# A new order for the same operations of an attention and feed-forward kernel, from the second product with w_in on

## The chip, the cores and the metric

The kernel runs on one core of a Trainium2 chip. The metric is the time of the slowest core in device microseconds, here that of the only core; several runs are taken and their median counts. A core has five engines with an instruction queue each: TensorE (PE, matrix products into PSUM banks), VectorE (DVE), ScalarE (ACT), GpSimd (POOL) and SyncE (SP, which here only issues DMAs).

## The reference

Attention without a softmax over pairs: q is normalised over its 64 elements, k over the 576 positions, and the product k·v of a head (64x64) is multiplied by q. What comes out is the input of a feed-forward layer with a softplus.

```
q_s = exp(q - max(q, -1));  q_s = q_s / (sum(q_s, -1) + 1e-09)        # (8, 8, 576, 64)
k_s = exp(k - max(k, 2));   k_s = k_s / (sum(k_s, 2) + 1e-09)
kv  = einsum('bhsd,bhse->bhde', k_s, v)
x   = einsum('bhsd,bhde->bhse', q_s, kv)  -> (4608, 512)
h   = x @ w_in                                                        # (512, 2048)
g   = maximum(h, 0) + log1p(exp(-abs(h)))
out = g @ w_out                                                       # (2048, 512)
```

## The kernel before

The 4608 tokens are nine tiles t of 512. Two heads are worked on together, so there are four head pairs h for each of the eight batches b. A full-precision product is made of three products of split operands: each operand is a high part (a cast to fp32r, which PE reads) and a low part (what the cast left), and high·high, high·low and low·high are added up in one PSUM bank. So a 128x512 product stands on PE three times in a row (L595 to L597 with w_in, L637 to L639 with w_out).

The work is cut into units, and each unit into numbered steps:

- `kv_unit` (token k*b.h.i*): maximum over positions on DVE (L336) and on PE or POOL, subtraction (L371, DVE), exp (L377, ACT), **exp(k)·v** (L387, PE: 10 narrow matmuls for one half, 20 for a head pair, into bank `att0` for even h and `att1` for odd h), then the scale 1/sum (L395 and L396, DVE), the high part of kv (L408, two on ACT) and its low part (L413, two on DVE).
- `q_unit` (q*t.i*): loaded by L432, maximum (L453), subtraction (L467), exp (L470, ACT), sums (L473, DVE, 128x1024), exchange of halves (L486, small copies), reciprocal (L496, L499), division (L502).
- `x_unit` (x*t.h.i*): transposition of q into the same `att` banks (L519, DVE), high part `q_hi` (L525, ACT), low part `q_lo` (L529, DVE), product with kv (L535 to L537, PE), then the split of the result for the next layer, or L547.
- U, A, H (or G), O: product with w_in into bank `ph` for one block j of 128 of the 2048 columns (L595 to L597), softplus (L604, ACT), split (L610 ACT, L613 DVE), product with w_out added into four banks `po` (L637 to L639). Tiles 0 to 2 are done in this plain way.
- Tiles 3 to 8 form three pairs p, and each pair of tiles is done with seven products where the plain way has eight: C (`pair_unit`, L722 to L724, with ACT at L734 to L742, DVE at L745 and L749, softplus at L752 and L756), d (`product_out`, L836 to L838) and the e, t, X steps that prepare operands (L816 and L819; L803; L679 to L686). These need sums of blocks of the weights, which the Y and y units make (L252 to L261, L280 to L289) and store (L265, L293).
- The split weights don't fit on chip with the rest: D (`keep_w`, L220) stores a block of 1 MB into DRAM, R0 (`fetch_w`, L224) fetches it again, R2 (L241) fetches sums.

What sets the order is a table written out by hand, the string `ORDER` at line 52: under a manual schedule the kernel runs through its tokens and each call `do(token)` issues that step's instructions. Every engine works off its own queue in this order and waits where an operand, a buffer or a bank isn't ready; all loads and most stores stand in SP's queue in the order of their tokens, and POOL's queue holds the last stores (L881). The buffers have names (w0 to w15, spare, x0 to x2, qt, kvt), and a tile that takes a buffer over waits for the last reader of the one before it. All tile names below carry a running number behind the name.

```
order = ORDER.split()
for token in order:
    do(token)
```

Of the kernel before, what the change touches and what calls it, by code (L numbers as in the profile page):

```python
# [1096 lines left out]
```

## Time and profile before

| | |
|---|---|
| time of the runs | 813.8 us median of 3 (813.17, 813.8, 814.79) |
| the profiled execution, span | 811.1 us |
| PE busy | 800.8 us, 99% |
| DVE busy | 625.9 us, 77% |
| ACT busy | 536.3 us, 66% |
| POOL busy | 115.1 us, 14% |
| DMA moved | 193.75 MB, mean 239 GB/s |

The profile is one execution. An engine's busy time is the time in which it executes something; matmuls are pipelined, so the durations of neighbours on PE overlap, and starts tell more than durations there. The list of waits gives for an engine what it stood idle for, and the timeline gives its instructions in a row, neighbours of one kind drawn together (x20 is 20 of them). Times count from the span's start.

### The profile page before, as it was taken

The numbers are of one execution on the slowest core, as the hardware profiler recorded it, in microseconds if no ns is written. First come the engines' busy times: TensorE is split into PE (matmuls) and PEld (weight loads), VectorE is DVE, ScalarE is ACT, GpSimd is POOL, SyncE is SP. The second block draws the span as 40 slices with busy tenths as digits, with TensorE's granted clock in tenths as the row PEclk, the third lists the DMA queues.
The fourth block names the chain that finished last, engine by engine and source line by source line (L and its number), as shares of the span: only waits on it lengthen the run. The fifth ranks groups of instructions, "written<-read, shape, count | busy, mean of one in ns | idle before, by whom it ended". The sixth has DMA issues, their size and how long they took to land.

```text
span 811.1 us, 12147 instructions
## 1 busy us (share of the span) xinstructions
PE 800.8 (99%) x4244; PEld 656.6 (81%) x4244; DVE 625.9 (77%) x1027; ACT 536.3 (66%) x868; POOL 115.1 (14%) x219
## 2 busy tenths in 40 slices
...
DVE  8888974569989999767889998767999922237983
...
PEclk9999999999999999999999999999999999999999
...
GB/s 340 373 273 182 59 39 274 267 176 385 401 279 257 328 337 343 340 372 253 139 324 237 186 115 265 275 270 93 280 201 197 178 261 198 175 156 322 211 126 70
DMA packets 114493, 193.75 MB, mean 239 GB/s; under 512 B 8000, under 2 KB 90176, under 8 KB 104192
## 3 DMA queue, kind: packets, MB, share of 16 engines
...
q10 hardware_dynamic: 320, 0.26, 0.1%
...
## 4 chain that ended last, share of the span: by engine, by line
PE 92%; DVE 3%; issue 2%; DMA 2%; SPq 1%; ACT 0%; POOL 0%; DVEq 0%; ACTq 0%; POOLq 0%
PE po L722 6%; PE po L838 6%; PE po L836 6%; PE po L837 6%; PE po L724 6%; PE po L723 6%; PE ph L595 5%; PE po L637 5%; PE ph L597 5%; PE ph L596 5%; PE po L638 5%; PE po L639 5%; PE ph L722 3%; PE ph L724 3%; PE ph L723 3%; PE ph L836 3%
## 5 line engine op out<-in xcount | busy, mean ns | idle before, releaser
L881 POOL DMA_DIRECT2D out<-w x92 | 59.3, 653 | 305.7 <-DVE w L873 304.4
L816 ACT CAST g_hi<-w 128x512 fp32r<-128x512 f32 x74 | 46.2, 624 | 31.1 <-PE ph L837 8.0
L595 PE MATMUL ph<-x,w 128*128 128x512 f32 x164 | 65.3, 398 | 1.1 <-DMA w<-kept 1.1
L637 PE MATMUL po<-w,g_hi 128*128 128x512 f32 x164 | 64.5, 394 | 0.0
L596 PE MATMUL ph<-x,w 128*128 128x512 f32 x164 | 64.0, 390 | 0.0
L597 PE MATMUL ph<-x,w 128*128 128x512 f32 x164 | 64.0, 390 | 0.0
L639 PE MATMUL po<-w,g_lo 128*128 128x512 f32 x164 | 64.0, 390 | 0.0
L638 PE MATMUL po<-w,g_hi 128*128 128x512 f32 x164 | 63.9, 390 | 0.0
L819 DVE TENSOR_TENSOR g_lo<-w,g_hi 128x512 fp32r<-128x512 f32 x74 | 51.0, 690 | 16.0 <-ACT g_hi L816 12.6
L803 DVE TENSOR_TENSOR w<-w,w 128x512 f32<-128x512 f32 x72 | 49.2, 686 | 5.3 <-ACT w L756 5.2
L752 ACT ACTIVATE w<-w 128x512 f32<-128x512 f32 x48 | 30.1, 632 | 34.8 <-DVE w L745 18.9
L745 DVE TENSOR_TENSOR w<-po,w 128x512 f32<-128x512 f32 x24 | 16.6, 690 | 46.9 <-PE po L724 46.3
L816 ACT CAST w<-w 128x512 fp32r<-128x512 f32 x52 | 32.2, 623 | 25.1 <-DVE w L819 8.1
L604 ACT ACTIVATE g<-ph 128x512 f32<-128x512 f32 x48 | 28.6, 599 | 29.8 <-PE ph L597 26.7
L722 PE MATMUL po<-w,x 128*128 128x512 f32 x112 | 44.1, 394 | 0.0
L724 PE MATMUL po<-w,x 128*128 128x512 f32 x112 | 43.7, 390 | 0.0
L723 PE MATMUL po<-w,x 128*128 128x512 f32 x112 | 43.7, 390 | 0.0
L610 ACT CAST g_hi<-g 128x512 fp32r<-128x512 f32 x46 | 28.6, 621 | 21.2 <-PE po L638 20.7
L613 DVE TENSOR_TENSOR g_lo<-g,g_hi 128x512 fp32r<-128x512 f32 x46 | 31.4, 683 | 12.6 <-ACT g_hi L610 12.4
L339 POOL PARTITION_ALL_REDUCE mx<-mx x20 | 17.2, 860 | 160.6 <-DVE mx L336 133.0
L336 DVE TENSOR_REDUCE mx<-kvt 128x128 f32<-128x640 f32 x28 | 36.9, 1319 | 2.5 <-DMA kvt<-in_kv_tail 2.5
L819 DVE TENSOR_TENSOR w<-w,w 128x512 fp32r<-128x512 f32 x52 | 35.6, 689 | 3.1 <-ACT w L816 1.0
...
## 6 DMA issues: line engine op xcount, KB each, us to landing
x<-sums SPq DMA_DIRECT2D x24, 1024.0 KB, 5.2
...
kept<-w SPq DMA_DIRECT2D x15, 1024.0 KB, 9.6
w<-kept SPq DMA_DIRECT2D x13, 1024.0 KB, 8.1
...
```

Of the source, the lines that this page charges most:

```text
L595: nc.tensor.matmul(ph, lhsT=w_hi, rhs=x_hi, start=h == 0, stop=False)
L596: nc.tensor.matmul(ph, lhsT=w_lo, rhs=x_hi, start=False, stop=False)
L597: nc.tensor.matmul(ph, lhsT=w_hi, rhs=x_lo, start=False, stop=h == HP - 1)
L637: nc.tensor.matmul(po, lhsT=g_hi[:, ms], rhs=w_hi, start=j == 0, stop=False)
L638: nc.tensor.matmul(po, lhsT=g_hi[:, ms], rhs=w_lo, start=False, stop=False)
L639: nc.tensor.matmul(po, lhsT=g_lo[:, ms], rhs=w_hi, start=False, stop=j == NJ - 1)
L722: nc.tensor.matmul(ph, lhsT=w_hi, rhs=x_hi, start=c == 0 and i in (0, 4), stop=False, **more)
L723: nc.tensor.matmul(ph, lhsT=w_lo, rhs=x_hi, start=False, stop=False, **more)
L724: nc.tensor.matmul(ph, lhsT=w_hi, rhs=x_lo, start=False, stop=c == 1, **more)
L816: nc.scalar.copy(ring[p, i, s][0], right_of(p, i, s))
L819: engine.tensor_tensor(out=lo, in0=right_of(p, i, s), in1=hi.bitcast(F32), op=ALU.subtract)
L836: nc.tensor.matmul(bank, lhsT=w_hi, rhs=hi, start=begin, stop=False, **more)
```

## The change

Only the string `ORDER` is replaced; no function, buffer or shape changes. Its first 58 tokens stand as before. Behind them the same tokens come in another order, but for twelve S tokens that issue nothing in the order before (they are left out). The new string is wrapped, which moves all lines of code behind it down by 149: L395 is L544 in the new file, L529 is L678, L224 is L373.

```
-    ... L1 k1.0.3 k1.0.4 U0 U1 k1.0.5 k1.0.6 k1.1.0 k1.1.1 J3 k1.0.7 A0 A1 O0 k1.1.2 P2 Q2 k1.1.3 x0.0.3 ...
+    k1.0.3 k1.0.4 U0 k1.1.0 U1 k1.0.5 A0 k1.0.6 J4 A1 J3 x0.2.3 x0.2.4 O0 P2 Q2 k1.0.7 x0.0.3 x0.1.3 x0.3.3 k1.1.1
```

Each engine has the same instructions in both, but for four table loads of ACT fewer. The runs of L387 on PE (matmuls of L387 with no other matmul between them) are 23 in the order before, nine of them with the two heads of neighbouring h in a row, and 19 in the new one, 13 of them with two.

Three places. First, SP's queue where block 3 of the weights is fetched into w3 (tiles kept2 and kept3 are the stored blocks, sums0 to sums3 the stored sums, kvt a load of k and v). Before:

```order
L224 DMA spare_2010<-kept1_1292 128x2048
L265 DMA sums1_2037<-w15_1711 128x2048
L241 DMA x2_2060<-sums0_1963 128x2048
L314 DMA kvt_2090<-in_kv 128x8x128
L318 DMA kvt_2090<-in_kv_tail 64x2x128
L224 DMA w2_2120<-kept2_1309 128x2048
L314 DMA kvt_2145<-in_kv 128x8x128
L318 DMA kvt_2145<-in_kv_tail 64x2x128
L224 DMA w3_2180<-kept3_1324 128x2048
```

Now:

```order
L373 DMA spare_1982<-kept1_1206 128x2048
L581 DMA qt_1987<-in_q 128x2048
L373 DMA w2_2018<-kept2_786 128x2048
L414 DMA sums1_2061<-w15_1438 128x2048
L414 DMA sums0_2076<-w1_1253 128x2048
L463 DMA kvt_2097<-in_kv 128x8x128
L467 DMA kvt_2097<-in_kv_tail 64x2x128
L463 DMA kvt_2103<-in_kv 128x8x128
L467 DMA kvt_2103<-in_kv_tail 64x2x128
L373 DMA w3_2185<-kept3_646 128x2048
L369 DMA kept15_2195<-w14_1138 128x2048
```

The fetch of kept2 into w2 stood between the two kvt loads of the batch; it now stands ahead of two stores of sums, and the two kvt loads are followed by w3 at once, with a store of w14 behind it.

Second, DVE at the x products of t=3 (q_lo is the low part of q, qt the q tile of t=4, s its sums, g_lo the low part of a softplus). Before:

```order
L529 TENSOR_TENSOR q_lo_2392<-att0_107,q_hi_2391 128x512
L473 TENSOR_REDUCE s_2253<-qt_1986 128x32
L371 TENSOR_TENSOR kvt_2313<-kvt_2313,mx_2396 128x10x64
L613 TENSOR_TENSOR g_lo_2416<-g_2398,g_hi_2415 128x512
L280 TENSOR_TENSOR w1_2428<-spare_2366 128x512
L473 TENSOR_REDUCE s_2253<-qt_1986 128x32
L529 TENSOR_TENSOR q_lo_2446<-att1_108,q_hi_2445 128x512
```

Now (L668 is L519, L678 is L529, L520 is L371, L762 is L613, L622 is L473):

```order
L429 TENSOR_TENSOR w14_2438<-w0_2325 128x512
L668 STREAM_TRANSPOSE att1_108<-w4_1737 128x512
L678 TENSOR_TENSOR q_lo_2460<-att0_107,q_hi_2459 128x512
L520 TENSOR_TENSOR kvt_2315<-kvt_2315,mx_2430 128x10x64
L762 TENSOR_TENSOR g_lo_2473<-g_2426,g_hi_2472 128x512
L438 TENSOR_TENSOR w12_2116<-w12_2116 128x1024
L678 TENSOR_TENSOR q_lo_2485<-att1_108,q_hi_2484 128x512
L622 TENSOR_REDUCE s_2057<-qt_1987 128x32
```

The two sums of q (L473) stood ahead of the second q_lo of this tile; now the first of them comes behind the fourth.

Third, DVE from the last kv products of b=4 to the first q_lo of t=4 (w5 is an operand of the first pair, w6 and w13 are sums of weights being made). Before:

```order
L395 TENSOR_SCALAR r_2789<-att0_107 128x1
L396 RECIPROCAL r_2789<-r_2789 128x1
L683 TENSOR_TENSOR w5_2775<-w4_1766,w5_2775 128x512
L395 TENSOR_SCALAR r_2814<-att1_108 128x1
L396 RECIPROCAL r_2814<-r_2814 128x1
L413 SCALAR_TENSOR_TENSOR kv_lo02_101<-att0_107,r_2789,kv_hi02_93 64x64 x2
L519 STREAM_TRANSPOSE att0_107<-qt_1986 128x512
L413 SCALAR_TENSOR_TENSOR kv_lo03_102<-att1_108,r_2814,kv_hi03_94 64x64 x2
L519 STREAM_TRANSPOSE att1_108<-qt_1986 128x512
L529 TENSOR_TENSOR q_lo_2828<-att0_107,q_hi_2827 128x512
```

Now (L832 is L683, L404 is L255, L429 is L280):

```order
L544 TENSOR_SCALAR r_2783<-att0_107 128x1
L545 RECIPROCAL r_2783<-r_2783 128x1
L562 SCALAR_TENSOR_TENSOR kv_lo02_101<-att0_107,r_2783,kv_hi02_93 64x64 x2
L668 STREAM_TRANSPOSE att0_107<-qt_1987 128x512
L832 TENSOR_TENSOR w5_2781<-w4_1737,w5_2781 128x512
L404 TENSOR_TENSOR w6_1785<-w6_1785 128x256
L544 TENSOR_SCALAR r_2833<-att1_108 128x1
L545 RECIPROCAL r_2833<-r_2833 128x1
L562 SCALAR_TENSOR_TENSOR kv_lo03_102<-att1_108,r_2833,kv_hi03_94 64x64 x2
L429 TENSOR_TENSOR w13_2843<-w0_2669 128x512
L668 STREAM_TRANSPOSE att1_108<-qt_1987 128x512
L678 TENSOR_TENSOR q_lo_2837<-att0_107,q_hi_2836 128x512
```

The second head's L395 and L396 stood right behind the first head's, one L683 between them; now they come behind the first head's L413 and L519, an L683 and an L255, and an L280 stands ahead of the second L519.

## Rows read from the trace of the kernel before

**Rows 1.** Page: busy time by engine, DVE in 40 slices, granted clock, chain.
```profile
PE 800.8 (99%) x4244; PEld 656.6 (81%) x4244; DVE 625.9 (77%) x1027; ACT 536.3 (66%) x868; POOL 115.1 (14%) x219
...
DVE  8888974569989999767889998767999922237983
...
PEclk9999999999999999999999999999999999999999
...
PE 92%; DVE 3%; issue 2%; DMA 2%; SPq 1%; ACT 0%; POOL 0%; DVEq 0%; ACTq 0%; POOLq 0%
```

**Rows 2.** PE's waits: tile, line, releaser, us in total, times, longest.
```profile
PE ph L595 <- DMA w<-kept: 1.1, 1, 1.1
```

**Rows 3.** Timeline of PE (start, duration, line, tiles) around a single and a pair.
```profile
57.77 0.39 PE L597 MATMUL ph<-x,w 128*128 128x512 f32 x1
...
59.15 0.40 PE L596 MATMUL ph<-x,w 128*128 128x512 f32 x1
...
144.45 0.39 PE L639 MATMUL po<-w,g_lo 128*128 128x512 f32 x1
144.77 1.39 PE L387 MATMUL att<-kvt 128*64 128x65 f32 x40
...
146.42 0.40 PE L596 MATMUL ph<-x,w 128*128 128x512 f32 x1
```

**Rows 4.** Timeline of PE around its two longest waits after the head.
```profile
232.43 0.39 PE L597 MATMUL ph<-x,w 128*128 128x512 f32 x1
233.89 0.47 PE L595 MATMUL ph<-x,w 128*128 128x512 f32 x1 [1.08 <-DMA w<-kept]
...
255.15 0.39 PE L639 MATMUL po<-w,g_lo 128*128 128x512 f32 x1
256.25 0.36 PE L535 MATMUL att<-q_hi,kv_hi 128*128 128x192 f32 x1 [0.71 <-DVE q_lo L529]
```

**Rows 5.** Timeline of SP's queue: start and end of one batch of loads.
```profile
218.57 0.55 SPq L314 DMA_DIRECT2D kvt<-in_kv  x1
...
224.82 0.85 SPq L224 DMA_DIRECT2D w<-kept  x1
```

**Rows 6.** Timeline of DVE ahead of the late L529.
```profile
254.39 1.21 DVE L473 TENSOR_REDUCE s<-qt 128x32 f32<-128x1024 f32 x1
255.52 0.68 DVE L529 TENSOR_TENSOR q_lo<-att,q_hi 128x512 fp32r<-128x512 f32 x1
```

**Rows 7.** Timeline of PE at two shorter waits.
```profile
490.92 0.39 PE L837 MATMUL po<-w,spare 128*128 128x512 f32 x1
491.44 0.51 PE L838 MATMUL po<-w,spare 128*128 128x512 f32 x1
...
534.65 0.39 PE L724 MATMUL ph<-w,w 128*128 128x512 f32 x1
535.40 1.40 PE L387 MATMUL att<-kvt 128*64 128x65 f32 x40 [0.36 <-issue]
```

**Rows 8.** Timelines of DVE, ACT, PE before the first x product of t=4.
```profile
289.22 0.16 DVE L395 TENSOR_SCALAR r<-att 128x1 f32<-128x1 f32 x1
...
293.10 0.69 DVE L529 TENSOR_TENSOR q_lo<-att,q_hi 128x512 fp32r<-128x512 f32 x1
...
290.55 0.63 ACT L408 ACTIVATE kv_hi<-att,r 64x64 fp32r<-64x64 f32 x2 [0.25 <-DVE r L396]
...
295.07 0.28 PE L535 MATMUL att<-q_hi,kv_hi 128*128 128x256 f32 x1
```

**Rows 9.** Groups of DVE by line: count, busy us, mean ns, idle before.
```profile
L255 DVE TENSOR_TENSOR w<-w 128x256 f32<-128x256 f32 x28 | 11.2, 424 | 0.0
...
L280 DVE TENSOR_TENSOR w<-w 128x512 f32<-128x512 f32 x11 | 7.5, 682 | 0.1
```

**Rows 10.** DMA issues, whole span and 470 to 500 us: KB, us to landing.
```profile
kept<-w SPq DMA_DIRECT2D x15, 1024.0 KB, 9.6
...
w<-in_q SPq DMA_DIRECT2D x1, 1024.0 KB, 6.9
```

More of the change, by code (lines that the diff above doesn't have):

```diff
@@ new lines @@
+    d0.5.0 x6.2.6 X1.0.hB22 X1.0.T3 t0.4.2 e0.5.4.0 e0.5.4.1 d0.5.1 e0.5.5.0 r0.12 x6.3.2 X1.0.lB22 R3.0.1 d0.5.2
+    o0.c11.1 e0.5.6.0 r0.13 e0.5.6.1 d0.5.3 X1.0.T2 e0.5.5.1 d0.5.4 t0.4.3 o0.c22.1 e0.5.7.0 e0.6.0.0 e0.6.0.1 d0.5.5
+    x6.3.3 X1.1.T1 X1.0.hT1 X1.1.hT1 x6.3.6 X1.1.hB22 R2.8 X1.0.lB21 e0.5.7.1 d0.5.6 e0.6.1.0 X1.1.T3 X1.1.lB22 d0.5.7
+    d0.6.0 X1.1.lT1 e0.6.1.1 d0.6.1 n e0.6.2.0 X1.0.lT1 C1.0.0 R3.1.1 e0.6.2.1 d0.6.2 o0.store.1.0 e0.6.3.0 e0.6.4.0
+    e0.6.5.0 e0.6.3.1 d0.6.3 X1.1.T2 o0.c12.0 e0.6.4.1 d0.6.4 R2.9 t0.4.6 X1.0.T4 e0.6.5.1 d0.6.5 X1.0.hT2 X1.1.hT2
@@ new lines @@
+    C1.1.11 C1.1.9 e1.0.1.0 C1.2.1 C1.2.8 C1.1.6 R4.5.1 q7.1 q7.12 k7.0.8 C1.0.16 C1.1.14 k7.2.0 k7.3.0 C1.2.2 C1.2.3
+    C1.3.0 C1.3.7 C1.2.4 R3.4.1 o0.store.2.1 C1.2.10 C1.2.11 C1.2.5 R2.12 o0.flip.2.0 o0.store.2.0 q7.2 C1.2.14 C1.2.9
+    C1.3.1 q7.4 C1.1.15 C1.3.8 q7.3 C1.2.6 o0.store.3.0 C1.2.15 k7.3.4 k7.3.5 k7.2.4 C1.3.2 R3.5.1 q8.0 k7.0.9 C1.3.3
+    C1.4.0 C1.3.4 o0.flip.1.1 k7.1.8 q8.1 k7.1.9 o0.store.1.1 C1.3.10 C1.3.11 C1.3.5 k7.2.5 k7.3.6 q7.5 k7.2.6 q7.7
+    C1.4.7 C1.4.1 k7.2.7 k7.3.7 q7.6 q7.8 k7.2.8 k7.2.9 q7.13 q7.9 q7.11 C1.3.6 R2.13 C1.4.2 C1.4.8 q8.12 q8.2 t1.1.2
@@ new lines @@
+    q7.10 C1.4.3 C1.3.9 o0.store.3.1 C1.2.16 C1.5.0 C1.4.4 C1.3.14 C1.4.10 C1.4.11 C1.5.7 C1.4.12 R4.7.1 x7.0.0 C1.4.5
+    C1.4.14 C1.5.1 C1.5.8 R4.4.1 C1.4.6 C1.3.15 C1.5.2 C1.4.9 C1.5.3 q8.3 k7.3.8 q8.4 q8.5 R3.6.1 C1.6.0 k7.3.9 C1.5.4
+    x7.0.1 x7.0.2 R2.14 x7.0.3 C1.5.10 C1.5.11 q8.7 q8.6 C1.5.9 C1.5.5 o0.store.0.0 C1.6.7 C1.6.1 R3.7.1 C1.5.6 x7.1.0
+    C1.3.12 x7.1.1 x7.1.2 R4.6.1 t1.1.1 q8.8 C1.6.8 C1.5.14 o0.store.0.1 x7.0.6 C1.6.2 C1.6.3 C1.7.0 C1.7.7 C1.4.15
+    C1.6.4 C1.6.9 t1.1.3 x7.1.3 C1.6.10 C1.6.5 x7.2.0 t1.1.4 R2.15 C1.7.1 r1.0 x7.2.1 x7.2.2 x7.2.3 C1.6.14 t1.1.6
@@ new lines @@
+    e1.4.4.1 d1.4.4 X2.0.hB22 e1.4.5.1 e1.4.7.0 d1.4.5 e1.4.6.1 d1.4.6 e1.4.7.1 d1.4.7 e1.5.0.0 r1.10 e1.5.0.1
+    e1.5.1.0 X2.0.T1 X2.0.T3 e1.5.3.0 d1.5.0 e1.5.1.1 e1.5.2.0 d1.5.1 X2.0.lB22 t1.4.1 o1.c11.0 e1.5.4.0 o1.c11.1
+    e1.5.2.1 d1.5.2 x8.3.3 o1.c22.1 e1.5.3.1 d1.5.3 e1.5.4.1 o1.c22.0 e1.5.5.0 X2.0.T2 e1.5.5.1 R2.16 X2.0.hT3
+    X2.0.lT3 x8.3.6 X2.1.hB22 e1.5.7.0 X2.1.lB22 X2.0.T4 X2.1.lB21 d1.5.4 d1.5.5 e1.5.6.0 e1.5.6.1 e1.6.0.0 e1.6.1.0
+    d1.5.6 e1.6.2.0 X2.1.T3 e1.5.7.1 X2.0.hT1 e1.6.0.1 r1.13 d1.5.7 o1.c12.0 e1.6.1.1 R3.0.2 e1.6.2.1 e1.6.3.0 R3.1.2
@@ new lines @@
+    X2.0.hT4 d1.6.0 d1.6.1 o1.c12.1 X2.0.hT2 X2.1.T2 X2.1.hT1 d1.6.2 e1.6.3.1 e1.6.4.0 e1.6.6.0 d1.6.3 e1.6.4.1
+    X2.1.hT3 X2.1.lT3 e1.6.5.0 e1.6.5.1 e1.6.7.0 d1.6.4 d1.6.5 X2.1.T4 X2.1.hT4 X2.1.lT4 R2.17 X2.1.hT2 e1.6.7.1
+    e1.6.6.1 o1.flip.3.0 X2.1.lT2 X2.0.lT1 C2.0.0 X2.0.lT2 C2.0.7 d1.6.6 d1.6.7 o1.c21.0 R4.0.2 C2.0.1 o1.c21.1
+    X2.1.lT1 C2.0.2 C2.0.8 R3.2.2 C2.0.3 C2.1.0 C2.0.4 C2.0.10 C2.0.11 C2.0.5 o1.flip.0.0 R4.2.2 C2.1.7 C2.0.14 C2.1.1
+    C2.1.8 X2.0.lT4 C2.0.9 C2.0.6 C2.0.15 C2.1.2 C2.1.3 R2.18 R3.3.2 C2.1.9 t2.1.0 C2.2.0 C2.1.10 C2.2.7 e2.0.0.0
@@ new lines @@
+    R4.1.2 C2.1.4 C2.1.11 C2.1.5 R4.4.2 C2.2.1 o1.flip.3.1 C2.2.8 C2.1.6 R2.19 C2.2.2 C2.2.9 R3.4.2 C2.2.3 C2.3.0
+    C2.2.4 o1.flip.2.1 C2.1.14 C2.1.15 C2.1.16 C2.2.10 C2.2.11 C2.3.7 C2.2.5 R2.20 o1.flip.1.0 C2.3.1 C2.3.8 C2.2.6
+    C2.3.2 R4.6.2 C2.3.3 C2.3.10 C2.4.0 C2.2.14 C2.4.7 C2.1.12 C2.3.4 C2.3.11 C2.3.5 o1.flip.1.1 R3.5.2 e2.0.0.1
+    C2.2.15 C2.4.1 R4.3.2 C2.3.6 C2.3.15 o1.flip.0.1 R2.21 C2.4.2 C2.4.8 C2.4.3 C2.0.16 o1.flip.2.0 C2.3.9 C2.3.12
+    C2.5.0 C2.4.9 C2.4.4 o1.store.2.1 C2.4.10 C2.4.11 C2.4.5 e2.0.1.0 C2.3.14 C2.5.7 C2.5.1 C2.4.6 C2.5.2 C2.5.8
@@ new lines @@
+    C2.5.3 C2.5.10 o1.store.3.1 C2.3.16 R3.6.2 C2.6.0 C2.4.15 C2.4.14 C2.6.7 C2.5.4 C2.5.11 R2.22 t2.1.2 R4.5.2 C2.5.5
+    e2.0.1.1 t2.1.1 C2.5.14 C2.5.12 C2.6.1 C2.5.9 R4.7.2 t2.1.3 C2.5.6 C2.6.2 o1.store.1.1 C2.6.8 C2.6.3 C2.6.10
+    R3.7.2 C2.7.0 C2.7.7 C2.6.4 e2.0.2.0 e2.0.3.0 R2.23 C2.6.5 C2.6.14 r2.0 e2.0.3.1 C2.7.1 C2.6.11 t2.1.5 C2.6.6
+    C2.7.2 C2.5.15 C2.6.9 C2.6.12 C2.7.8 C2.7.3 o1.store.1.0 d2.0.0 e2.0.4.0 C2.7.4 C2.7.10 C2.7.5 e2.0.4.1 d2.0.1
+    C2.4.12 e2.0.5.0 C2.7.11 C2.7.12 r2.11 C2.7.6 e2.0.2.1 C2.7.15 d2.0.2 e2.0.6.0 C2.6.15 d2.0.3 C2.7.9 e2.0.7.0
@@ new lines @@
+    C2.7.16 r2.1 r2.2 d2.0.4 e2.3.0.0 e2.0.5.1 C2.4.16 d2.0.5 e2.3.1.0 e2.0.6.1 d2.0.6 C2.0.12 e2.3.2.0 C2.2.16 r2.3
+    e2.3.0.1 e2.0.7.1 d2.0.7 t2.1.4 o1.store.0.0 C2.5.16 e2.3.1.1 r2.5 e2.3.2.1 C2.2.12 t2.2.2 o1.store.2.0 t2.3.2
+    t2.1.6 d2.3.0 t2.2.1 C2.7.14 o2.spread.0 d2.3.1 d2.3.2 e2.3.3.0 e2.3.3.1 d2.3.3 t2.2.3 e2.3.4.0 e2.3.4.1 e2.3.5.0
+    e2.3.5.1 t2.2.5 t2.1.7 e2.3.6.0 e2.3.6.1 t2.2.0 e2.3.7.0 d2.3.4 r2.4 d2.3.5 e2.3.7.1 o1.store.0.1 e2.1.0.0
+    e2.1.1.0 d2.3.6 e2.1.2.0 e2.1.0.1 d2.3.7 r2.7 o2.v.0 t2.2.4 r2.6 o2.spread.1 d2.1.0 t2.3.1 e2.1.1.1 d2.1.1 t2.2.6
```

110 lines of the change are left out of this document (109 added, 1 removed).

## The prediction

> **What bounds the kernel now.** The page comes first. PE is busy 800.8 of 811.1 us and the chain of work that ended last is 92% PE [rows 1], so the time is the sum of what PE executes plus the few places at which PE waits; nothing on another engine counts unless PE waits for it. The granted clock is in its top tenth in all 40 slices [rows 1], so no clock term enters. The DVE slices say where a new wait would arise: DVE stands at 9 in six of the seven slices from 182 to 324 us and at 4 to 7 in the four slices ahead of these [rows 1]. The list of PE's waits is the second view: it names a DMA in front of L595 as the longest outside the head [rows 2], and next a DVE operation in front of L535 [rows 4]. The timeline of PE is the third; there I read starts, since matmuls overlap: a 128x512 product starts 0.23 us after the one before it when nothing is wrong, and whatever exceeds that is lost time.
>
> **The runs of exp(k)·v.** A run of 20 narrow matmuls (one head's L387) costs more than its own work, because the steps into it and out of it are longer than 0.23. A single: from L597 at 57.77 to the second product behind the run, L596 at 59.15, is 1.38 us; less two normal steps of 0.23 that leaves 0.92. Two heads back to back (x40): 144.45 to 146.42 is 1.97, less 0.46 leaves 1.51 [rows 3]. Two singles cost 1.84, a pair 1.51, so each merge saves 0.33. On PE the order has 23 runs of L387 before (9 of them pairs) and 19 after (13 pairs): four merges, at PE work, so no other engine's work hides them. **−1.3 us.** The work of the runs is unchanged: each engine issues the same instructions, except that ACT loads its table four times less, and ACT is not in the chain. That gives nothing by itself.
>
> **Stalls that the new order takes away.** Four places.
> (a) L597 starts at 232.43, the next L595 at 233.89: 1.46, that is 1.23 too much, and its releaser is the fetch of w3 [rows 4]. SP begins the batch that holds it at 218.57 with a kvt load and gets to w3 only at 224.82; w3 is there 9 us later [rows 5]. Ahead of w3 stand two kvt loads and the 1 MB of w2. In the new order w2 is asked for earlier, ahead of two stores of sums, so SP gets to w3 sooner and 1 MB less is under way with it. About 3.2 MB took the 15.2 us from 218.57 to 233.8; at that pace (an estimate) 1 MB less is 4.8 us, four times the wait. PE needs w3 as many products behind the kvt releases as before. What was late next there is the kvt itself, which no view shows as waited for. I take all of it, **−1.2** (0 to −1.2; the end at zero if the stores, now close ahead, cost as much as the load did).
> (b) L639 at 255.15, L535 at 256.25: 1.10, so 0.87 too much, waiting for q_lo, L529 [rows 4]. That L529 starts on DVE only at 255.52, because two L473 of 1.21 us with L371, L613 and L280 between them stand in the queue behind the L529 before it; the second L473 ends its place there [rows 6]. The new order has no L473 between the transposes of these heads and their L529, and the sums of q fall behind the fourth one. **−0.9** (0 to −0.9).
> (c) L838 at 491.44 starts 0.52 after L837 and the next step is 0.34 as well: 0.4 too much, waiting for an L819 of DVE [rows 7]. (d) L387 at 535.40 starts 0.75 after L724; the step into such a run is 0.32 at 144.45, so 0.43 too much, with 0.36 of it put down to issue; the operand is ACT's exp, L377 [rows 7, 3]. In the new order other work stands ahead of both producers, so the same wait isn't due; that none takes its place I can't show. **−0.8** together (0 to −0.8).
> Sum of what goes: 1.3 + 1.2 + 0.9 + 0.8 = **−4.2 us**.
>
> **Waits that the new order brings.** The list of DVE work ahead of a PE instruction is compared at each such place, with durations from the rows.
> (e) The first x product of t=4. Before, the pair of k runs starts at PE 24 products ahead of L535, and DVE goes from the first L395 at 289.22 to L529 at 293.10, which ends at 293.79; PE gets to L535 at 295.07, so 1.3 us are to spare [rows 8]. In the new order L255 (0.42) and L280 (0.68) have come in between [rows 9]. The second head's L395 and L396 come behind L519, L683 and L255 instead of ahead of them, so ACT's L408 of that head (0.63 for the two) can no longer run beside the first head's L413 and L519: DVE waits for it. In the queue, where back-to-back starts lie some 0.08 closer than the durations (1.13 apart for 1.21 in [rows 6]), that is L683 0.60 (moved in from a gap in which DVE waited anyway), L255 0.34, L395 and L396 0.4, the wait 0.7, L280 0.60: 2.6 us. L529 then ends at about 296.4, 1.3 behind the need. If DVE gets to the first L395 early, part of it is hidden; I take **+1.1** (0 to +1.4).
> (f) Two more places have less room than before: the g_lo, L613, behind the sums of q for t=1 (near 170 us; two L473 of 1.21 and four small copies ahead of it), and ACT's L679 into w6, which now follows a store of sums out of w6, near 290 us. Neither waits in this trace. The waits of this kind that it does show are between 0.4 and 0.9 [rows 4, 7]; I take the lower end for each, **+0.8** (0 to +1.8).
> (g) The q load of t=7 (L432 into w4). SP issues it behind the 1 MB of x2, and its first reader, L453, now stands on DVE right ahead of L395, L396 (twice) and the L745 that empties bank po2. PE comes back to po2 48 products and a pair after the release of x2: 48·0.23 + 1.5 = 12.5 us. Behind the landing come L453 1.2, four small ones 0.6 and L745 0.6. So PE waits only if the load takes over 12.5 − 0.4 − 2.4 = 9.7 us. It took 6.9 in this trace, but kept<-w took 9.6 in its median [rows 10]. I take **+0.2** (0 to +1.5).
> The Trainium skill, page "DMA: Bandwidth & Descriptors", section Measured, gives 6.15 us for 1 MB. The trace's 6.9 for the same load agrees roughly, its 9.6 does not, and by the page alone (g) would be zero and the sum 0.2 us lower.
> Sum of what comes: +2.1 (0 to +4.7). A gain from these three is excluded, since PE waits at none of them now.
>
> **The net.** −4.2 + 2.1 = −2.1 us against the profiled execution's own 811.1 us. That is 2.7 below the median 813.8 of the runs, for what lies around the span; the change doesn't touch that, so it is carried over: 813.8 − 2.1 = **811.7 us**.
>
> **The rivals.**
> 1. All stalls go, none comes: −4.2, **809.6 us**. For it: DVE may reach (e) early, since sum units that stood at 180 to 324 us now begin before 180, where DVE has room. Against it: the chain at (e) is counted instruction by instruction and needs the room to be 1.3 larger.
> 2. The gains are eaten: merges −1.3 and one of (a) and (b) stay, but (e), (f) and (g) come near their upper ends, or the stores of sums that now precede the w3 batch hold it. −1.3 − 1.2 + 2.5 gives about **813.8**, no change. For it: DVE has no slice of rest from 182 to 324 us, so what is pulled out of one place is pushed into another. Against it: part of that work does leave the crowded stretch.
> 3. Slower, by one mechanism: a DVE instruction that waits for a load holds back everything queued behind it, among it the operation that empties a PSUM bank. The place is (g). From a landing of 9.7 us on each us goes straight onto PE's path, and nothing later gives it back, since the load is not asked for earlier than x2's release. To end 1.6 us above 813.8 it must eat the 2.1 as well: a landing of 9.7 + 0.2 + 2.1 + 1.6 = 13.6 us, **815.4 us and more**; with two loads of kvt and the x0 sums under way at the time this would be half as long again as the 9.6 of [rows 10]. For it: L453 is placed directly in front of the L745. Against it: no 1 MB load has a median near 13 us in the page.
> The Trainium skill, page "Perfetto Trace Analysis", section Tensor Engine Instruction, calls DVE and ACT strict FIFO. The late L529 behind L473 in [rows 6] agrees; by that rule DVE can't step over the waiting L453, and a late landing ends in rival 3's 815.4.
> That the change doesn't do what it says is no case here: the 19 runs can be counted in the order.
>
> **How the numbers follow.** Chances: the forecast with its mix of waits (810.4 to 812.9) 0.45; rival 1 (809 to 810.4) 0.20; rival 2 (812.9 to 815.4) 0.26; rival 3 0.09. About 0.2% or 1.6 us is what a measurement of this kernel can tell from no change, so faster means below 812.2, slower above 815.4. Of the forecast's 0.45 some three quarters lie below 812.2: faster 0.34 + 0.20 = 0.54, same 0.11 + 0.26 = 0.37, slower 0.09. The range starts at 809.2, which is rival 1 with another 0.4 for places I didn't see, and ends at 814.6, inside rival 2; outside lie rival 3 and thin ends of 1 and 2.
>
> **What would show it.** In the new trace: 13 x40 islands of L387 on PE, each about 1.5 us; no wait for w<-kept in front of L595 near 230 us; no wait of L535 on q_lo near 255; one of about 1 us at the first L535 of t=4, near 292 us, put down to DVE L529; a DVE idle stretch, if any, at L453 near 500 us put down to w<-in_q. The prediction is wrong if PE shows a wait of over 1 us at a place not named here, if (e) shows none, or if the w3 wait is still there.

## The result: slower, by new waits of PE, most of them at places that the prediction had not compared

The new order takes **822.4 us** (median of five, 820.59 to 823.25) where the old one, on the same chip, takes 814.2 (813.17 to 815.15): a ratio of 1.0096, interval 1.0079 to 1.0112. It is 8.2 us slower; the forecast was 2 us faster. The profiled execution has a span of 818.7 us against 811.1, and that difference of 7.6 is what the trace can explain. The execution profiled is the fastest of the five (820.59); the spread between executions makes up the rest.

The page of the changed kernel, where the rows answer to [rows 1]: busy time by engine, DVE in 40 slices, granted clock and the chain.

```profile
PE 803.4 (98%) x4244; PEld 655.1 (80%) x4244; DVE 623.4 (76%) x1027; ACT 520.2 (64%) x864; POOL 115.7 (14%) x219
...
DVE  8879874788889889885689997685798841237874
...
PEclk9999999999999999999999999999999999999999
...
PE 79%; DVE 8%; ACT 5%; DMA 3%; issue 3%; POOL 1%; SPq 0%; DVEq 0%; ACTq 0%; POOLq 0%
```

DVE and ACT are busy a little less than before, PE 2.6 us more, and no slice has a lower clock. What changed is the chain: 92% PE has become 79%, with 8% on DVE and 5% on ACT. PE stands and waits. The list of PE's waits (tile, line, releaser, us in total, times, longest) is complete here; only the first row, in the head, and L1045 at the end also stand in the trace of before.

```profile
PE ph L1187 <- DVE ident L269: 3.0, 1, 3.0
PE po L788 <- DVE g_lo L762: 2.4, 2, 1.3
PE att L684 <- DVE q_lo L678: 1.8, 1, 1.8
PE po L871 <- DVE w L894: 0.8, 1, 0.8
PE po L871 <- ACT w L905: 0.8, 1, 0.8
PE ph L745 <- DVE w L356: 0.5, 1, 0.5
PE po L1045 <- DVE w L1038: 0.5, 1, 0.5
PE ph L744 <- ACT g L753: 0.4, 1, 0.4
```

The DMA wait of [rows 2] is gone, and so is the wait for q_lo of [rows 4]. In their place stand waits for DVE and ACT, and none of them is for a transfer. Idle time in the list understates them, since matmuls overlap, so I add up starts on PE instead, step by step, in both traces:

| from the starts on PE, us | before to after |
|---|---|
| the stalls (a) to (d) | −2.9 |
| four merges of k runs | −1.3 |
| eleven new stalls, each over 0.15 (below) | +8.8 |
| the step behind a break (0.34 for 0.23), ten more of them | +1.1 |
| some 3030 ordinary steps, 0.2 ns longer in the mean | +0.6 |
| tail behind the last product | +0.8 |
| rest | +0.4 |
| sum (span: +7.6) | +7.5 |

The eleven, by PE's start and with what each exceeds a normal step: 102.2 (0.70), 117.0 (1.47), 180.9 (1.22), 227.8 (0.58), 296.5 (1.99), 380.9 (0.32), 382.2 (0.91), 438.1 (0.16), 447.7 (0.27), 543.2 (0.92), 577.1 (0.29). Four show the kinds.

*At 117: two engines in each other's way.* Timelines of PE, DVE and POOL (start, duration, engine, line, tiles, and idle time before it with its releaser):

```profile
116.97 0.40 PE L787 MATMUL po<-w,g_hi 128*128 128x512 f32 x1
118.67 0.50 PE L788 MATMUL po<-w,g_lo 128*128 128x512 f32 x1 [1.30 <-DVE g_lo L762]
...
116.12 3.10 DVE L762 TENSOR_TENSOR g_lo<-g,g_hi 128x512 fp32r<-128x512 f32 x2 [1.80 <-ACT g_hi L759]
...
115.64 2.42 POOL L356 TENSOR_TENSOR w<-w,w 128x1024 fp32r<-128x1024 f32 x1 [2.18 <-ACT w L354]
```

Two L762 need 1.3 us elsewhere; here they take 3.10, the first of them 2.50: it ends 0.56 behind POOL's L356, which ends at 118.06, so most of its 0.68 of work was still to be done then. POOL's operation stands at this time in the old order too (115.22), but there the DVE operations that start while it runs have one operand in PSUM, and take their usual 0.68 to 0.73. In the new order a g_lo, with both operands in SBUF, has come there.

*At 296.5: place (e) of the prediction.* PE, then DVE, where r, L562, L668 and L678 are the chain to the first x product of t=4 ([rows 8] before):

```profile
289.83 1.39 PE L536 MATMUL att<-kvt 128*64 128x65 f32 x40
...
296.50 0.39 PE L788 MATMUL po<-w,g_lo 128*128 128x512 f32 x1
298.71 0.35 PE L684 MATMUL att<-q_hi,kv_hi 128*128 128x256 f32 x1 [1.83 <-DVE q_lo L678]
...
291.25 0.16 DVE L544 TENSOR_SCALAR r<-att 128x1 f32<-128x1 f32 x1
...
292.37 0.58 DVE L562 SCALAR_TENSOR_TENSOR kv_lo<-att,r,kv_hi 64x64 fp32r<-64x64 f32 x2 [0.76 <-ACT kv_hi L557]
...
295.92 0.58 DVE L562 SCALAR_TENSOR_TENSOR kv_lo<-att,r,kv_hi 64x64 fp32r<-64x64 f32 x2 [0.76 <-ACT kv_hi L557]
...
297.88 0.69 DVE L678 TENSOR_TENSOR q_lo<-att,q_hi 128x512 fp32r<-128x512 f32 x1
```

From the first r to L678 DVE takes 6.63 us where it took 3.88, 2.75 more. It also reaches that r 1.42 us behind the start of the pair instead of 1.04, since a 1.23 us division and a 0.68 us sum of weights stand ahead. Of these 3.1 us, the 1.3 that were to spare cover a part.

*At 382 and 543: a bank is emptied late.* PE twice, then ACT ahead of the second:

```profile
383.22 0.50 PE L871 MATMUL po<-w,w 128*128 128x512 f32 x1 [0.79 <-DVE w L894]
...
544.33 0.50 PE L871 MATMUL po<-w,w 128*128 128x512 f32 x1 [0.76 <-ACT w L905]
...
541.36 1.00 ACT L589 COPY other<-m 32x64 f32<-32x64 f32 x4
542.38 1.28 ACT L905 ACT_TABLE_LOAD   x1
543.68 0.60 ACT L905 ACTIVATE w<-po 128x512 f32<-128x512 f32 x1
```

At 543 the L905 that empties the bank stands behind four small copies (1.00) and its table load (1.28); at 382 the L894 that empties it starts 1.81 us behind the start of a q_lo that waited 0.51 for ACT, with a g_lo and two kv_lo between them. The other larger ones are of the same sort: at 102 DVE's split of block 13 (L356) stands behind three other operations, at 181 the g_lo behind a 1.23 us division (place (f)), at 228 a softplus behind a table load and a kv_hi that waited for DVE. The four small ones (381, 438, 448 and 577, 1.0 together) are left without a cause here.

### The profile page after: what moved, and what is told of

The parts are those of the page before. It is cut to its first block, busy times and chain, and to the rows that moved or that the text cites. A ratio compares the mean times of both kernels' runs of the same rounds, so it can differ in the third digit from the quotient of the medians.

```text
span 818.7 us, 12087 instructions
## 1 busy us (share of the span) xinstructions
PE 803.4 (98%) x4244; PEld 655.1 (80%) x4244; DVE 623.4 (76%) x1027; ACT 520.2 (64%) x864; POOL 115.7 (14%) x219
## 4 chain that ended last, share of the span: by engine, by line
PE 79%; DVE 8%; ACT 5%; DMA 3%; issue 3%; POOL 1%; SPq 0%; DVEq 0%; ACTq 0%; POOLq 0%
PE po L987 7%; PE po L985 7%; PE po L986 7%; PE po L871 5%; PE po L872 5%; PE po L873 5%; PE ph L744 4%; PE ph L746 4%; PE ph L745 4%; PE po L788 3%; PE po L786 3%; PE po L787 3%; PE ph L871 3%; PE ph L872 3%; PE ph L873 3%
## 5 line engine op out<-in xcount | busy, mean ns | idle before, releaser
L894 DVE TENSOR_TENSOR w<-po,w 128x512 f32<-128x512 f32 x24 | 16.6, 691 | 40.7 <-PE po L873 40.3
L488 POOL PARTITION_ALL_REDUCE mx<-mx x20 | 19.4, 971 | 182.6 <-DVE mx L485 164.5
L762 DVE TENSOR_TENSOR g_lo<-g,g_hi 128x512 fp32r<-128x512 f32 x46 | 33.2, 730 | 15.3 <-ACT g_hi L759 15.2
L871 PE MATMUL po<-w,x 128*128 128x512 f32 x112 | 44.1, 394 | 0.1
L788 PEld LDWEIGHTS po<-w,g_lo 128*128 128x128 f32 x164 | 30.8, 188 | 10.2 <-DVE g_lo L762 3.9
L745 PEld LDWEIGHTS ph<-x,w 128*128 128x128 f32 x164 | 30.8, 188 | 6.9 <-DVE w L356 1.0
```

Of the source, the lines that this page charges most:

```text
L745: nc.tensor.matmul(ph, lhsT=w_lo, rhs=x_hi, start=False, stop=False)
L788: nc.tensor.matmul(po, lhsT=g_lo[:, ms], rhs=w_hi, start=False, stop=j == NJ - 1)
L871: nc.tensor.matmul(ph, lhsT=w_hi, rhs=x_hi, start=c == 0 and i in (0, 4), stop=False, **more)
```

## The experiments

The theory: DVE and ACT work off their queues in order, with under about 1 us of room at dozens of places, and the new order has put other work ahead of instructions for which PE waits. Rivals: one cause makes most of the loss (the port at 117, or place (e)); DVE simply has too much to do, and no order helps; PE, freed of its old waits, meets the next late instruction by itself, whichever order. The diffs show only the tokens that move. T, J, P, Q are steps of making and splitting a block of w_in or w_out, Q0.1 the low part of block 0 on POOL; R0 is a fetch, D a store, U, A, G, O, H the plain product and its softplus, C a pair unit, Y and y sums of weights. Spans are those of the profiled executions.

**Eight repairs in the new order, each with the wanted instruction ahead in its queue.** The diff shows four of them; the other four move a few tokens each at 228, 380, 543 us and at the end.

```diff
-T15 J15 D9 k1.2.9 x1.0.0 P13 Q13 x1.1.0
+T15 P13 J15 Q13 D9 k1.2.9 x1.0.0 x1.1.0
-Q15.1 P0 G13 G14 x1.1.4 x1.1.5 x1.3.0 x1.2.3 Q0.1
+Q15.1 G13 G14 x1.1.4 x1.1.5 x1.3.0 x1.2.3 P0 Q0.1
-k2.2.9 q2.10 x2.0.0 D14 H1.7.1
+k2.2.9 H1.7.1 q2.10 x2.0.0 D14
-R0.11 q4.11 Y5.1 R0.12 X0.0.hB11 k4.2.7 X0.1.hB11 k4.2.8 k4.2.9 x4.0.0 ...
+R0.11 R0.12 X0.0.hB11 k4.2.7 k4.3.7 X0.1.hB11 k4.2.8 k4.3.8 k4.2.9 x4.0.0 k4.3.9 q4.11 ...
...
```

> The new order with eight local repairs, each a few tokens moved past one another so that the instruction PE stood waiting for comes ahead of what stood in front of it on DVE or ACT: the split of block 13 before the kv steps (stall at 102 us, 0.8), the POOL split of block 0 behind two g_lo (117 us, 1.6), g_lo ahead of the division of q (181, 1.3), the scales of a k pair ahead of the division (228, 0.7), both scales together and the sums behind the x product (296, 2.0), q's exchange and division behind L894 (381 to 383, 1.2), q's exchange behind the softplus (543, 1.0), the last POOL stores in their old order (tail, 0.8). Theory of place (each stall is one instruction that stands too late in a queue): the stalls add up to 9.4 us and go, 822.4 - 9.4 = 813, within 1.5. Rival of crowding (DVE and ACT have too much to do in those stretches, whatever the order): the waits reappear within some us of each repaired place and the time stays above 818.

Measured: 816.96 us, 1.0037 (1.0025 to 1.0049), span 814.1. The stalls that were repaired are gone, and others have come: 122.0 (0.72), 200.1 (0.87), 298.4 (1.13), 384.7 (0.86) are the larger of nine, 5.45 us together (0.6 of it is two small ones that were not repaired, at 448 and 577 before). The tail is 0.75 shorter again. Its list of PE's waits:

```profile
PE ph L1187 <- DVE ident L269: 3.0, 1, 3.0
PE att L684 <- DVE q_lo L678: 3.0, 5, 1.0
PE ph L744 <- ACT g L753: 0.7, 1, 0.7
PE po L1045 <- DVE w L1038: 0.5, 1, 0.5
```

Place in the queue is a true cause, worth 4.6 us of span; half of what the repairs freed was met again a little later, now nearly all in front of q_lo. The time lies between what the two theories had.

**The two largest alone.** Block 0's low part on DVE instead of POOL, and, in another kernel, the old order of the steps around (e).

```diff
-x1.2.3 Q0.1 P1
+x1.2.3 Q0 P1
```

> The new order with one change: the low half of the split of block 0 (L356 on POOL, 2.42 us from 115.64) runs on DVE. Theory of the port: the L762 that started at 116.12 and took 2.50 us instead of 0.68 was held by the POOL instruction with two SBUF operands; without it it takes 0.68 and the wait of L788 at 117 us goes (1.5 of time, less what 1.2 us more on DVE cost elsewhere). Rival, a late cast on ACT: L762 still ends near 118.6 and the wait of about 1.3 us stays.

Measured in one execution: span 819.0 (818.7). DVE at the place:

```profile
116.75 1.29 DVE L762 TENSOR_TENSOR g_lo<-g,g_hi 128x512 fp32r<-128x512 f32 x2 [1.80 <-ACT g_hi L759]
```

Without the operation on POOL the same two take 1.29 for 3.10, so that was the mechanism, and the wait at 117 is gone; but PE waits 0.84 at 122.6 instead. This execution is 0.6 late at 102 us already, ahead of the edit; counted from there it is 0.4 shorter, of the 1.5 that went.

```diff
-R0.11 q4.11 Y5.1 R0.12 X0.0.hB11 k4.2.7 X0.1.hB11 k4.2.8 k4.2.9 x4.0.0 ...
+R0.11 R0.12 X0.0.hB11 k4.2.7 k4.3.7 X0.1.hB11 k4.2.8 k4.3.8 k4.2.9 x4.0.0 k4.3.9 q4.11 ...
```

> The new order with the steps around the first x product of t=4 alone put back: both heads' scales right behind one another, the division of q and the sums (L401, L404, L429 and the like) behind the first q_lo. Theory of place: the wait of 2.0 us in front of L684 near 297 goes and the trace is some 2 us shorter, all else as before. Rival of crowding: the wait comes back at one of the next three x products or at L788 within 10 us, and the time falls by less than 1.

Measured in one execution: span 818.9. PE passes (e) without a break and stops 3.2 us later, for the next pair of heads (and 0.76 at 517.7, far behind the edit; more on that below):

```profile
296.84 0.39 PE L788 MATMUL po<-w,g_lo 128*128 128x512 f32 x1
297.06 0.28 PE L684 MATMUL att<-q_hi,kv_hi 128*128 128x256 f32 x1
...
300.27 0.39 PE L746 MATMUL ph<-x,w 128*128 128x512 f32 x1
301.47 0.39 PE L684 MATMUL att<-q_hi,kv_hi 128*128 128x256 f32 x1 [0.81 <-DVE q_lo L678]
```

Neither of the two largest makes the loss.

**The old order with its own three waits taken away.** w2 asked for earlier, so that w3 can come earlier; the sums of q behind the second q_lo; two divisions of q behind the exps.

```diff
-Y6.1 R0.1 q3.1 ... q3.7 R0.2 k3.0.8
+Y6.1 R0.1 R0.2 q3.1 ... q3.7 k3.0.8
-O35 q4.8 x3.1.1 x3.0.6 x3.1.2 q4.13 k4.1.0
+O35 x3.1.1 x3.0.6 x3.1.2 q4.8 q4.13 k4.1.0
-k7.3.4 q7.13 C1.3.6 ... q7.9 C1.3.15 k7.3.5 k7.2.6 q7.10
+k7.3.4 C1.3.6 ... C1.3.15 k7.3.5 k7.2.6 q7.13 q7.9 q7.10
```

> The kernel before with three of its own four stalls taken away by moving a few tokens: the fetch of w2 asked for right behind the one before it (w3 stall, 1.24), the second sum of q behind q_lo of the second head (0.87), the exchange of q behind the two exps (0.43). If the gains of the prediction were sized right, the three waits are gone and the time is 2.5 us lower, 811.7; if the fetch was not late because of w2, the wait at L595 near 233 us stays and the gain is about 1.3.

Measured: 816.86 us, 1.0038 (1.0026 to 1.0051): slower, though each edit was meant only to take a wait away. The wait at 233 is gone, and PE waits 1.89 at 250.5 and 1.26 at 259.7 instead, 0.5 each at 296 and 300, and behind the third edit 0.92 at 542.8 (for ACT) and 0.48 at 546.6. DVE of this kernel, then of the kernel before:

```profile
227.97 1.32 DVE L336 TENSOR_REDUCE mx<-kvt 128x128 f32<-128x640 f32 x1 [3.68 <-DMA kvt<-in_kv_tail]
```

```profile
226.77 1.34 DVE L336 TENSOR_REDUCE mx<-kvt 128x128 f32<-128x640 f32 x1 [2.50 <-DMA kvt<-in_kv_tail]
```

The 1 MB asked for earlier lies ahead of the kvt loads: they land 1.2 us later and DVE waits so much longer. From there on it runs that much behind: the q_lo that PE waits for at 250.5 starts at 251.86 instead of 250.72, while PE, with the wait at 233 gone, comes to it 1.1 us earlier. DVE is busy 39.3 of the 40 us from 240 to 280 (39.5 in the old order), so there is little room to catch up. That the stalls at 233 and 255 in the trace of before are one shortage of DMA, seen at two engines, fits this but is not shown: in the next experiments each of them goes while the other stays.

**Less work on DVE.** Four kernels that leave out the 64 additions of L255 and L283, which add up blocks of the weights (so their results are not those of the reference): old order, old order with the edits for w3 and q_lo, new order, new order with the eight repairs.

```diff
-Y0.2 Y0.3 Y0.4 Y0.5 y0.2 y0.3 y0.4 y0.5
...
-Y7.2 Y7.3 Y7.4 Y7.5 y7.2 y7.3 y7.4 y7.5
```

> The kernel before without the 64 additions of weight blocks in the sum units (L255 and L283, some 56 of them on DVE, 23 us of its busy time between 180 and 330 us; the sums come out wrong, nothing else changes). Crowding: DVE's own wait in front of L535 (0.87 near 255) goes, the DMA wait at L595 near 233 (1.24) stays, the time falls by about 1. Place: the same, as one of the additions' neighbours stands ahead of that L529; this kernel is the yardstick of the next ones.

> The kernel before without the 64 additions, and with two of its stalls taken away as in b_three (w2 fetched early; the second sum of q behind q_lo). Crowding: with DVE unloaded the gains come through: no wait over 0.3 between 225 and 305 us, some 1.2 below the light kernel before. If the waits of 1.9 and 1.3 near 251 and 260 are still there, they are made by the place of an instruction and not by DVE's load.

> The new order without the 64 additions. Crowding: the waits in DVE's full stretch go (228: 0.6, 297: 2.0, and most of 181: 1.2), those at 102, 117, 381 and 543, outside it, stay: the time falls by 3 to 4, to about 818.5. Place: the wait at 297 falls only by the one L404 that stands in its chain (0.34), the others stay, the time falls by under 1.

> The new order with the eight repairs and without the 64 additions. Crowding: of the waits left with the repairs those at 200 and 298 (0.9, 1.1) go, and the time comes to some 814.5, level with or below the light kernel before. Place: they stay, about 816.5.

| | with the additions | without |
|---|---|---|
| old order | 814.2 | 812.23, 0.9975 (0.9963 to 0.9987) |
| old, w3 and q_lo edits (with: the divisions too) | 816.86 | 814.47, 1.0003 (0.9994 to 1.0013) |
| new order | 822.4 | 818.43, 1.0050 (1.0035 to 1.0065) |
| new, eight repairs | 816.96 | 813.98, 0.9999 (0.9990 to 1.0009) |

The columns are from different chips, on which the old order's medians differ by up to 0.4 us. Lighter DVE gives back 2 to 4 us, more in the new order, and there it takes the stalls at 181, 200 and 298 away and halves (e) (1.99 to 1.01). It leaves those at 102, 117, 228, 381, 382 and 543 as they are. So both act: DVE's load, and the place in the queue. Between the two orders place is the larger: without the additions the new order is still 6.2 us behind the old one (8.2 with them), and with the repairs 1.8. In the old order lighter DVE takes the wait at 255 away and leaves that at 233 (1.21). With the edits for w3 and q_lo waits of 1.24 at 250.9 and 1.26 at 259.4 stay, and DVE stands 5.44 us for the kvt: there the late load makes them, not the work of DVE.

**The parts of the change in the old order.** Eight stores of split weights asked for 30 to 90 us earlier, so that the DMA is emptier at 180 to 230 us; and three of the four merges.

```diff
-U18 D2 U19 D3 ... A18 U20 D4 ... U21 D5 ... U22 D6 ... U23 D7 ... H1.7.0 D8 ... x2.0.1 D9
+U4 D3 ... Q7 D4 ... U7 D2 ... A7 D7 ... A9 D5 U10 D6 ... U12 D8 ... U13 D9
```

> The kernel before with eight of the sixteen stores of weight blocks (L220, 1 MB each) asked for some 30 to 90 us earlier, where the DMA queues are near empty; nothing else moves. Theory of bytes: between 180 and 230 us the loads and stores are what is full (380 to 414 GB/s), kvt lands late there, DVE idles 2.5 us for it and has no room afterwards to make it up, so PE's waits at 233 (1.24) and 255 and 260 (1.0) are one shortage. With 8 MB gone from the stretch DVE's idle 2.5 us for kvt near 224 shrinks to under 0.5, all three waits go and the time falls by 2.2, to 811.6. Rival, order in DVE's queue: the DMA wait at 233 goes (1.2) but those of L535 stay or grow, and the time falls by under 1.

Measured: 812.42 us, 0.9984 (0.9975 to 0.9994). The wait for w3 is down from 1.23 to 0.20 without any fetch moved; the kvt is there 0.5 us earlier; 0.80 at 254.7 stays. The DMA moves 361 and 357 GB/s from 180 to 200 and 200 to 220 us instead of 384 and 414. The profiled execution is one of the slower ones, though (813.64, span 811.6, no shorter than the old order's): in it PE waits 0.70 at 294.3 and 0.49 at 298.5 as well, behind a sum of weights (L252) for which DVE stood 1.82 us until a block was fetched. So the gain is in the times, and where it lies this trace doesn't show. This is the fastest order found, 1.1 us ahead of the old one and, by the two ratios, about 9 ahead of the new.

```diff
-k1.2.5 k1.2.6 M11.1 ... k1.2.7 k1.3.4 k1.3.5 Q9 U9 k1.3.6
+k1.2.5 M11.1 ... k1.3.4 k1.3.5 Q9 U9 k1.2.6 k1.3.6 k1.2.7
-k4.0.6 q4.10 x3.3.3 ... y1.6 k4.1.6
+q4.10 x3.3.3 ... y1.6 k4.0.6 n k4.1.6
-k6.0.6 C0.7.7 ... q6.12 k6.1.6
+C0.7.7 ... q6.12 k6.0.6 n k6.1.6
```

> The kernel before with three of the four merges alone (k1.2 with k1.3, k4.0 with k4.1, k6.0 with k6.1: the first head's product put right ahead of the second's). If a merge is worth 0.33 and brings nothing else: three runs fewer on PE, 1.0 us less, 813.2. If two heads at once make bursts on DVE and ACT that PE then waits for, new waits appear within 10 us of the merged pairs (near 85, 268, 399 us) and the time is level or up to 1 above.

Measured: 818.61 us, 1.0071 (1.0059 to 1.0084), span 816.3. Read by starts, the merges are worth 0.95 us, 0.32 each, as forecast. But at the first of them DVE's r, now right behind the pair, waits for PE, and the split of the next block waits behind r. DVE, then PE:

```profile
85.58 0.16 DVE L395 TENSOR_SCALAR r<-att 128x1 f32<-128x1 f32 x1 [4.13 <-PE att L387]
...
88.12 1.22 DVE L207 TENSOR_TENSOR w<-w,w 128x1024 fp32r<-128x1024 f32 x1
...
86.04 0.49 PE L595 MATMUL ph<-x,w 128*128 128x512 f32 x1
89.39 0.50 PE L596 MATMUL ph<-x,w 128*128 128x512 f32 x1 [2.86 <-DVE w L207]
...
91.42 0.63 PE L597 MATMUL ph<-x,w 128*128 128x512 f32 x1
91.84 0.63 PE L595 MATMUL ph<-x,w 128*128 128x512 f32 x1
```

That costs 3.1 us, and a further 1.6 because the products behind it start 0.43 apart; more on that below. With the early stores added (the two edits together, of which a line each):

```diff
-U18 D2 U19 D3 ... k1.2.5 k1.2.6 M11.1
+U4 D3 ... U7 D2 ... k1.2.5 M11.1
```

> The kernel before with both the earlier stores of eight weight blocks and the three merges: 811.6 - 1.0 = 810.6 if the two add, and 811.6 or above if the merges bring waits of their own.

Measured: 817.67 us, 1.0057 (1.0045 to 1.0070), with the same 2.86 us wait: the two effects stand side by side.

**Can the new order be mended?** Two more rounds, of five and of three repairs, each at the stalls that the round before had left.

```diff
-q1.11 x1.1.2 ... P0 Q0.1 P1 x1.3.1 ... k3.1.0 q3.2 x2.1.0
+x1.1.2 q1.11 ... P0 Q0.1 x1.3.1 P1 ... x2.1.0 k3.1.0 q3.2
...
```

> The new order with the eight repairs and five more for the waits that came in their place (108: 0.7, 122: 0.7, 200: 0.9, 298: 1.1, 385: 0.9, together 4.3): if these were again single instructions that stand too late, 812.7; if the shortage only moves on, about 815 with new waits of the same sum elsewhere.

```diff
-x1.1.2 q1.11 x1.1.3 Q14 P15 ... y5.1 y5.2 ... x4.2.2 A44
+x1.1.2 x1.1.3 Q14 q1.11 P15 ... x4.2.2 y5.1 y5.2 y5.3 y2.6 A44
...
```

> The new order with thirteen repairs and three more (the split of block 14 ahead of the division of q at 110 us, 0.6; the softplus of its block ahead of the casts of sums at 301, 1.0; sums behind the q_lo at 305 and 309, 0.5 and 0.7): 2.8 in all, 813.0, if single instructions are late; 815 or more, with new waits of the same sum, if the order has no room left.

Measured: 815.85 (1.0033, 1.0021 to 1.0044) and 815.45 (1.0021, 1.0013 to 1.0030). Against the old order on the same chip the new one stands at +8.2, then +3.1, +2.4 and +1.7 us. The last one's waits, besides the head and L1045:

```profile
PE att L684 <- DVE q_lo L678: 1.6, 3, 1.1
PE po L871 <- DVE w L894: 1.5, 2, 1.3
...
```

Of the 1.5 at L871, 1.3 are new, at 515 us, where no repair was made. That is place (g) of the prediction. DVE there, ahead of the L894 that PE waits for:

```profile
514.11 1.22 DVE L602 TENSOR_REDUCE m<-w 128x32 f32<-128x1024 f32 x1 [7.84 <-DMA w<-in_q]
```

In this execution, the slowest of the eleven (817.03), the load of q took 10.80 us. The 0.76 at 517.7 in the kernel with (e) alone put back is the same wait, with a load of 10.14. The other waits that each round leaves are at new places.

**Can the old order be bettered by more than the stores?** The early stores, the sums of q behind the second q_lo and two sums of weights later; then the merges of b=4 and b=6 as well.

```diff
-H2.8.0 Y5.0 Y6.6 Y4.8 H2.8.1 Y5.1 Y6.7 O39 A41 y5.0 R0.11 k4.3.0 Y5.2
+H2.8.0 Y6.6 Y4.8 H2.8.1 Y6.7 O39 A41 y5.0 R0.11 k4.3.0 Y5.0 Y5.1 Y5.2
```

> The kernel before with the eight stores of weight blocks asked for earlier (b_spread), the second sum of q behind the q_lo of its neighbour (wait of 0.8 at 255), and the sum of block 11 (L252, which held DVE 1.8 us for a fetch near 278 and so L529 at 294 and 298: 0.7 and 0.5) some steps later. If these are three single causes the waits at 255, 294 and 298 go and it is 2.0 below b_spread's 812.4: 810.4. If DVE's stretch from 240 to 300 us is simply full, the waits come back within 20 us and it stays at 812 or above.

```diff
-k4.0.6 q4.10 x3.3.3 ... y1.6 k4.1.6
+q4.10 x3.3.3 ... y1.6 k4.0.6 n k4.1.6
...
```

> The same with two of the merges (k4.0 with k4.1, k6.0 with k6.1), those that brought no wait of over 0.5 near 268 and 399 when they were made alone: 0.32 each, 0.6 below b_best0. If merging two heads costs DVE and ACT what it saves PE: level with b_best0 or above, with a wait within 10 us behind one of the pairs.

Measured: 816.56 (1.0039, 1.0024 to 1.0054) and 818.12 (1.0051, 1.0037 to 1.0065). Both are slower. In the first, PE loses 2.4 at 294.8 for q_lo and 1.4 in the middle of a pair for an exp; in the second that one is 2.3:

```profile
289.38 0.80 PE L387 MATMUL att<-kvt 128*64 128x65 f32 x20 [2.10 <-ACT kvt L377]
```

The exp is late by the edit itself. The two sums of weights (L252) now stand behind the fetch R0.11 and read block 11 from the copy that is being fetched into `spare`; DVE stands still for it, and the L371 on which the exp waits is queued behind. DVE of the first:

```profile
285.14 0.69 DVE L252 TENSOR_TENSOR w<-spare 128x512 f32<-128x512 f32 x1 [4.77 <-DMA spare<-kept]
...
287.03 0.82 DVE L371 TENSOR_TENSOR kvt<-kvt,mx 128x640 f32<-128x640 f32 x1
```

In the second DVE stands 3.44 us at the same L252. So these two kernels don't tell whether the old order has room from 240 to 300 us: the edit moved a sum, and made it wait for another copy of its operand.

## Why the prediction was wrong

**The runs of exp(k)·v: right.** 13 pairs and 6 singles, 1.3 us less, and 0.32 per merge in the old order too, against 0.33 from [rows 3].

**Stalls that go: right.** None of (a) to (d) is left; forecast 2.9, found 2.9. For (a) the mechanism can be checked too: in the new order SP asks for w3 2.7 us behind the first kvt load (222.05 and 224.72) instead of 6.25, and w3 is there 8.1 us later, 10.8 us behind that kvt load instead of 15.2. That is 4.4 less where the estimate had 4.8. That the two stores of sums close ahead of this batch don't hold it was right as well. What the text called late next, the kvt, was the right suspect: in the old order an earlier fetch makes it late (the old order with its own three waits taken away).

**Waits that come: the step that failed.** It stood at +2.1 (0 to +4.7) and is +8.8 for the stalls, with 1.1 for the steps behind them and 0.8 in the tail.
- (e) had the right place and mechanism and the wrong size: 1.99 for 1.1. The longer chain was counted nearly right (2.75 for 2.6); what was missing is that DVE reaches it 0.4 later than before, behind a division and a sum. I had set the possibility that it gets there earlier as the only open side. The 2.75 has ACT's answer in it twice, 0.76 each.
- (f) was 1.22 at one place and nothing at the other, for 0.4 each.
- (g) came on DVE and not on PE. DVE stands for the load as the prediction's last paragraph said, and L894 ends 0.6 us before PE needs it:

```profile
515.62 1.22 DVE L602 TENSOR_REDUCE m<-w 128x32 f32<-128x1024 f32 x1 [5.84 <-DMA w<-in_q]
```

  The load took 8.81 us. The forecast let PE wait from 9.7 us on, and the other traces of the new order bear that out: at 8.1 to 9.4 us (five of them) PE doesn't wait, at 10.14 and 10.80 it loses 0.76 and 1.42. So this price was right, and whether it is paid changes from one execution to the next.
- The other stalls, 5.6 us together, stand at places that the text doesn't name. It compared the queues "at each such place", but did so only where something in the diff had drawn my eye; at 102, 117, 228, 382 and 543 the same comparison was open to be made. For most of these it would have been the plain count of (e). For 117 it would not: the 2.50 us of an operation that takes 0.68 stood in no row that I had read, and the order lists each engine by itself.

**The rivals.** Rival 3 had the side right and, for this trace, the mechanism wrong: its mechanism is there (DVE at (g), above), but none of the eleven stalls stands behind a load. Elsewhere it does reach PE: at (g) in two other traces of the new order, and at the L252 of the last two kernels. Rival 2 had the mechanism nearly (what is pulled out of one place is pushed into another), but let it end at no change, for no reason: nothing bounds it there. The evidence against it, that work leaves the crowded slices, was true and did not help: DVE is busy 127.0 of the 142 us from 182 to 324 instead of 135.5 and stands at 9 in two of those seven slices instead of six, and PE loses 0.58 (at 227.8) and 1.99 (at 296.5) there all the same.

**The range** held the sum's known unknowns. It lacked the one that decided: how many of the places where PE meets DVE or ACT have less than 1 us to spare, out of all that the change reorders.

**The 2.7 us around the span** are 1.9 to 2.1 in every execution for which both are listed (813.17 and 811.1 in the old order, 820.59 and 818.7 in the new). The rest is the spread of the executions, and the difference doesn't depend on it.

**What stays open.** How the 8.8 us divides between load and place: the two act on the same stalls (without the additions −3.9, with the repairs −5.0, with both −8.4). Set against an old order that is lightened too, load makes 2.0 of the 8.2 and the rest is place. The port and place (e) alone were measured in one execution each, without an interval. Only the fastest of the five executions of the new order has a trace, so what makes the others up to 2.7 us longer is open. No run here tells whether a fourth round of repairs would bring the new order below the old.
